# ScalarE copies the first product into the next bank, TensorE adds on top; running sums copied out by ScalarE, accumulators emptied in halves

## The chip, the cores and the metric

The kernel runs on 1 core of one Trainium2 chip. The metric is device time in microseconds (us) of one execution. The engines are TensorE (PE; its weight loads are listed as PEld), VectorE (DVE), ScalarE (ACT), GpSimd (POOL) and SyncE (SP), which issues DMAs. PE writes its products into PSUM, which is used here as eight banks of 128 x 512 fp32: `b0` to `b3` and `o0` to `o3`.

## The reference

Attention with squared ReLU scores over 8 x 3072 tokens, then two mixtures of 8 experts. The change touches only the first mixture, in which every token goes through all experts:

```
x = attn_out.reshape(B * S, D)            # 24576 x 256
logits = x @ w_gate                       # 24576 x 8, then exp and 8 rounds of normalising
for e in range(E):                        # E = 8, F = 1024
    h = np.maximum(x @ w1[e], 0.0)        # 24576 x 1024
    ye = h @ w2[e]                        # 24576 x 256
    out += P[:, e:e + 1] * ye
```

The second mixture routes each token to one expert by an argmax over `x @ emb`; its routing starts while the first mixture still runs.

## The kernel before

All large products are done with fp16 operands split into a high and a low part (three matmuls: high x high, high x low, low x high). The work runs in three stages: attention, the mixture of all experts, the mixture with routing. The middle stage has 768 units. A unit is one expert, two tiles of 512 tokens (1024 tokens) and one quarter of the 1024 hidden features.

**First layer.** `x @ w1` of a unit is a 2 x 2 block product done with seven block products instead of eight (lines 897 to 953). Each block product is three matmuls of 512 columns into one bank. `unit_head` makes four: A11 into `r0`, S1 into `r2`, S2 into `r1`, A22 into `r3`. `unit_tail` makes three more: A12 is added onto `r0`, S4 onto `r2`, S3 onto `r1`. Banks `r0` to `r3` are `b0` to `b3`. ScalarE copies A11 out as `c1` (L920) and S1 as `s5` (L922); VectorE forms the running sums `u2` = S2 + c1 (L926) and `u3` = S2 + S3 + c1 (L946); blocks of the result are `r0`, `c12` = r2 + u2 (L943), and the two halves of `blocks`: r3 + u3 on VectorE (L953) and s5 + u3 on GpSimd (L952). ScalarE applies ReLU and gives the high half in fp16 (L940, L944, L958), VectorE the low half (`low`, L933). A12 and S4 give the part `f0` of the hidden features, `blocks` gives the part `f1`.

**Second layer.** `unit_second(k, q)` multiplies part `q` with `w2`: 24 matmuls of 256 columns into four accumulators `o0` to `o3` (L969), three for each of eight token groups. After the last quarter of the features (`p == 3`) the accumulators are emptied: `evac_begin` has ScalarE read `o0` and `o2` (L1236), `evac_end` has VectorE read `o1` and `o3` (L1252) and GpSimd add what ScalarE copied (L1254).

**Order.** Every engine works through its queue in the order in which the program is written; nothing is rescheduled. The loop over units (L1477 to L1515) is pipelined by one unit: on TensorE stand, in this order, the head of unit k+1 (12 matmuls), the second layer of part `f0` of unit k (24), the tail of unit k+1 (9), the second layer of part `f1` of unit k (24).

**Background.** At four ticks per unit small pieces of other work are put into the queues: normalising of the gates (`sinkhorn`), the routing of finished tiles (`tile_end`), splitting of weights and tiles. One tick stands inside the head, after S1, through the argument `between`. Only this tick may put small products on TensorE, and all of them go to bank `b3`, which `r3` uses too: `pl` (the logits, read by ScalarE at L1123), `pr` (ranks, read by VectorE at L1157 and L1158), `pc` (column sums, read by VectorE at L1035). In L1083 ScalarE squares a finished tile, for which it needs the sum that GpSimd made in L1254.

Of the kernel before, what the change touches and what calls it, by code (L numbers as in the profile page):

```python
# [4 lines left out]
F32 = mybir.dt.float32  # L5
F16 = mybir.dt.float16
I32 = mybir.dt.int32
AF = mybir.ActivationFunctionType
ALU = mybir.AluOpType
AX = mybir.AxisListType  # L10

P = 128
D = 256
E = 8
# [3 lines left out]
TOK = 512  # L18
# [4 lines left out]
SB = 4  # L23
A12, A22, S1, S2, S3, S4, A11 = range(7)
# [62 lines left out]
def program(tc, u, v, z, wg, w1a, w2a, emb, tau, w1b, w2b, out, pool, psum, dram):  # L87
# [575 lines left out]
    with tc.manual_schedule():  # L663
# [167 lines left out]
        def attn_main(i):  # L831
# [24 lines left out]
            if b == B - 1 and qc == QC - 1 and n == 0:  # L856
                load_expert(0)

        moe(tc, dict(locals()))


def moe(tc, st):
# [9 lines left out]
    ones16, ones32, tri16, iota8, half, tokid, itau, emb, out = (  # L872
        g[k] for k in "ones16 ones32 tri16 iota8 half tokid itau emb out".split()
    )
    PE, ACT, DVE, POOL, SP = nc.tensor, nc.scalar, nc.vector, nc.gpsimd, nc.sync
# [3 lines left out]
    terms = []  # L879
    o_ps = {}  # L880
# [3 lines left out]
    def hl_part(i):  # L884

        if not halves:
            t = pool.tile([P, 2, 2, 2 * TOK], F16, name="hl2", tag="z8", bufs=1)
            halves.extend(t[:, j] for j in range(2))
            halves.extend(t.rearrange("p b a q -> p (b a q)").rearrange("p (a q) -> p a q", a=2) for t in hls)
        return halves[i % 4]  # L890

    def product(r, k, blk, part, c, start):
        i, e, p = units[k]
        w = W[i // SB * E + e][0][p // 2]
        x = X[i // 2][part][:, c // 2, c % 2]
        for j, (a, b) in enumerate(((0, 0), (0, 1), (1, 0))):
            PE.matmul(  # L897
                r, lhsT=w[:, p % 2, blk, a, :], rhs=x[:, b, :], start=start and j == 0, stop=j == 2,
                skip_group_check=True,
            )  # L900

    def unit_head(k, between=None):

        i, e, p = units[k]
        sb, t = divmod(i, SB)
        if not terms:
            terms.append(m4([P, 2, TOK], F32, "terms"))
            terms.append(m4([P, 2, TOK], F32, "blocks"))
            terms.append(small("prod5", TOK))
        if i // 2 not in X:  # L910
            bg.finish("x")
        n = sb * E + e
        if t == 0 and p == 1 and n + 1 < NTILE // SB * E:
            load_expert(n + 1)
        if sb + 1 < NTILE // SB and p == 1 and (e, t) in ((4, 0), (7, 2)):
            bg.add("x", load_pair_of_tiles((i + SB) // 2))
        r = live[k] = [bank(j, f"r{j}") for j in range(3)]
        c1, u2, s5 = terms[0][:, 0], terms[0][:, 1], terms[2]
        product(r[0], k, A11, 0, 0, True)
        ACT.activation(out=c1, in_=r[0], func=AF.Copy)  # L920
        product(r[2], k, S1, 1, 0, True)
        ACT.activation(out=s5, in_=r[2], func=AF.Copy)  # L922
        if between:
            between()
        product(r[1], k, S2, 1, 3, True)
        DVE.tensor_tensor(out=u2, in0=r[1], in1=c1, op=ALU.add)  # L926
        r.append(bank(3, "r3"))
        product(r[3], k, A22, 1, 1, True)

    h0, h1 = slice(0, TOK), slice(TOK, 2 * TOK)  # L930

    def low(dst, src, hi, eng=DVE):
        eng.scalar_tensor_tensor(out=dst, in0=src, scalar=0.0, in1=hi, op0=ALU.max, op1=ALU.subtract)  # L933

    def unit_tail(k):

        r = live[k]
        f0, c1, c12 = hl_part(2 * k), terms[0][:, 0], terms[0][:, 1]
        product(r[0], k, A12, 0, 1, False)
        ACT.activation(out=f0[:, 0, h0], in_=r[0], func=AF.Relu)  # L940
        product(r[2], k, S4, 0, 3, False)
        low(f0[:, 1, h0], r[0], f0[:, 0, h0])
        DVE.tensor_tensor(out=c12, in0=r[2], in1=c12, op=ALU.add)  # L943
        ACT.activation(out=f0[:, 0, h1], in_=c12, func=AF.Relu)  # L944
        product(r[1], k, S3, 1, 2, False)
        DVE.tensor_tensor(out=c1, in0=r[1], in1=c1, op=ALU.add)  # L946
        low(f0[:, 1, h1], c12, f0[:, 0, h1])

    def unit_sums(k):
        r = live.pop(k)  # L950
        u3 = terms[0][:, 0]
        POOL.tensor_tensor(out=terms[1][:, 1], in0=terms[2], in1=u3, op=ALU.add)  # L952
        DVE.tensor_tensor(out=terms[1][:, 0], in0=r[3], in1=u3, op=ALU.add)  # L953

    def unit_split(k):
        c2 = terms[1].rearrange("p h q -> p (h q)")
# [1 line left out]
        ACT.activation(out=f1[:, 0], in_=c2, func=AF.Relu)  # L958
        low(f1[:, 1], c2, f1[:, 0])

    def second(hl, f, n, w2t, b0=0):

        for t in range(n // P):
            b = b0 + t // 2
            if f == 0 and t % 2 == 0:
                o_ps[b] = psum.tile([P, 2 * D], F32, name=f"o{b}", tag=f"o{b}", bufs=1)
            o = o_ps[b][:, t % 2 * D:(t % 2 + 1) * D]
            for a, h in ((0, 0), (0, 1), (1, 0)):
                PE.matmul(  # L969
                    o, lhsT=hl[:, a, t * P:(t + 1) * P], rhs=w2t[:, f, h * D:(h + 1) * D],  # L970
                    start=f == 0 and t % 2 == 0 and a + h == 0, stop=f == 7 and a == 1, skip_group_check=True,
                )

    def unit_second(k, q):
        i, e, p = units[k]
        second(hl_part(2 * k + q), 2 * p + q, 2 * TOK, W[i // SB * E + e][1])


    state = {"gates": False}
# [207 lines left out]
    accs = {}  # L1187
# [23 lines left out]
            state["done", i] = True  # L1211
            yield

    parts = []

    def gate(i, e, t):
        return None if i < SB and e < 3 else L[:, 4 * i + t, e:e + 1]

    def target(i, e):

        if e == 0:
            accs[i] = buffer(i)
        elif i < SB and e < 3 and (i, e) not in accs:
            accs[i, e] = buffer(i + SB) if e == 1 else m4([P, 4, D], F32, "y")
        return (accs[i, e] if 0 < e < 3 and i < SB else accs[i]), e == 0 or (i < SB and e < 3)

    def evac_begin(i, e):

        for h in range(2):
            y, new = target(i + h, e)  # L1230
            if not new:
                s = pool.tile([P, TOK], F32, name="r", tag="r", bufs=3).rearrange("p (t d) -> p t d", t=2)
                parts.append((y, s))
            for t in range(2):
                c = gate(i + h, e, t)
                ACT.activation(  # L1236
                    out=y[:, t] if new else s[:, t], in_=o_ps[2 * h][:, t * D:(t + 1) * D], func=AF.Copy,
                    scale=1.0 if c is None else c,
                )

    def evac_end(i, e):
        for h in range(2):
            y, new = target(i + h, e)
            for t in range(2, 4):
                o = o_ps[2 * h + 1][:, (t - 2) * D:(t - 1) * D]
                c = gate(i + h, e, t)
                if c is None:
                    DVE.tensor_copy(out=y[:, t], in_=o)
                elif new:
                    DVE.tensor_scalar(out=y[:, t], in0=o, scalar1=c, scalar2=None, op0=ALU.mult)  # L1250
                else:
                    DVE.scalar_tensor_tensor(out=y[:, t], in0=o, scalar=c, in1=y[:, t], op0=ALU.mult, op1=ALU.add)  # L1252
        for y, s in parts:
            POOL.tensor_tensor(out=y[:, 0:2], in0=y[:, 0:2], in1=s, op=ALU.add)  # L1254
        parts.clear()
        if e == E - 1:
            for h in range(2):
                bg.add("end", tile_end(i + h, accs[i + h]))


    tab = {}
# [74 lines left out]
    def finish_tiles():  # L1336
        bg.finish("end")
# [102 lines left out]
    for k in range(ns):  # L1440
        if k == ns - 120:
            bg.add("prep", embeddings())
        end = (k + 1) % KT == 0
# [33 lines left out]
    for k in range(nu):  # L1477
        i, e, p = units[k]
        if (i, e, p) == (SB, 0, 0):
            g["depth"][0] = 2  # L1480
            bg.lane_rate("w", 6)
            g["plan_weights"](1)
        if i >= NTILE - SB and e == E - 1 and p % 2:
            bg.finish("w")
            if TOK not in tab:
                finish_tiles()
            j = i - (NTILE - SB) + p // 2
            if j < 3:
                load_job_weights(j)
            if i == NTILE - 2 and p == 1:  # L1490
                load_job_rows(0)
        if k + 1 < nu:
            unit_head(k + 1, (lambda: tick_misc(k - 1)) if k else None)
        else:
            for j in range(3, AHEAD_W):
                load_job_weights(j)
            job_first(0)
        unit_split(k)
        unit_second(k, 0)
        tick()  # L1500
        if k + 1 < nu:
            unit_tail(k + 1)
        else:
            job_first(1)
        tick()
        unit_second(k, 1)
        if p == 3:
            evac_begin(i, e)
        if k + 1 < nu:
            unit_sums(k + 1)  # L1510
        else:
            job_first(2)
        if p == 3:
            evac_end(i, e)
        tick()  # L1515


# [39 lines left out]
```

## Time and profile before

| | us |
|---|---|
| median of 3 runs | 10601.97 (10598.34 to 10606.39) |
| profiled execution, its own time | 10603.76 |
| its span, first to last instruction | 10602.0 |
| PE busy | 10453.1 (99%) |
| DVE busy | 6783.1 (64%) |
| ACT busy | 4462.1 (42%) |
| POOL busy | 3512.3 (33%) |
| the 41640 second-layer matmuls, L969 (both mixtures) | 4890.6 busy, 0.9 idle before them |
| the 16128 first-layer matmuls, L897 | 3756.5 busy, 29.1 idle before them |

The granted TensorE clock was 0.996 of full speed over the span. Idle time of an engine is charged to the instruction that comes after it, and to the engine that released that instruction. A busy share of PE says nothing on how fast a matmul runs, so the idle time is what is read here.

### The profile page before, as it was taken

The numbers are of one execution on the slowest core, as the hardware profiler recorded it, in microseconds if no ns is written. First come the engines' busy times: TensorE is split into PE (matmuls) and PEld (weight loads), VectorE is DVE, ScalarE is ACT, GpSimd is POOL, SyncE is SP. The second block draws the span as 40 slices with busy tenths as digits, with TensorE's granted clock in tenths as the row PEclk, the third lists the DMA queues.
The fourth block names the chain that finished last, engine by engine and source line by source line (L and its number), as shares of the span: only waits on it lengthen the run. The fifth ranks groups of instructions, "written<-read, shape, count | busy, mean of one in ns | idle before, by whom it ended". The sixth has DMA issues, their size and how long they took to land. (4 is left out here: it accounts for less than half of the span.)

```text
span 10602.0 us, 193662 instructions
## 1 busy us (share of the span) xinstructions
PE 10453.1 (99%) x78492; PEld 7454.5 (70%) x78492; DVE 6783.1 (64%) x11720; ACT 4462.1 (42%) x8092; POOL 3512.3 (33%) x3094
## 2 busy tenths in 40 slices
PE   8999999999999999999999999999999999999999
PEld 6777777766666666666666666666666666666678
DVE  7676666676667666676766767666666666753333
ACT  5555555334434444443444434344343444433223
POOL 4444445333233333323333323333223332322111
PEclk9999999999999999999999999999999999999999
DMA  8998998311112111111211212112121111115556
GB/s 206 222 224 212 223 222 202 102 38 48 57 52 64 56 58 54 58 58 51 64 56 46 76 42 63 58 49 70 50 53 57 48 47 51 44 62 166 168 186 206
DMA packets 1133187, 1024.67 MB, mean 97 GB/s; under 512 B 853152, under 2 KB 990624, under 8 KB 1102464
## 3 DMA queue, kind: packets, MB, share of 16 engines
q1 hardware_dynamic: 1113520, 960.62, 33.3%
q0 software_dynamic: 18768, 51.67, 1.4%
q8 instruction: 613, 10.04, 0.4%
q14 instruction: 286, 2.34, 0.1%
HBM read 594.27 MB, written 223.93 MB: 77 GB/s over the span
## 5 line engine op out<-in xcount | busy, mean ns | idle before, releaser
L969 PE MATMUL o<-w2t,hl 128*128 128x256 f16 x41640 | 4890.6, 273 | 0.9 <-DVE hl L933 0.6
L969 PEld LDWEIGHTS <-hl 128*128 128x128 f16 x41640 | 4073.8, 98 | 863.1 <-issue 2.1
L897 PE MATMUL r<-xs,w1t 128*128 128x512 f16 x16128 | 3756.5, 379 | 29.1 <-DVE blocks L953 16.9
L952 POOL TENSOR_TENSOR blocks<-prod,terms 128x512 f32<-128x512 f32 x768 | 1336.6, 1740 | 4833.8 <-ACT hl L944 4833.3
L897 PEld LDWEIGHTS <-w1t 128*128 128x128 f16 x16128 | 1567.7, 98 | 1594.1 <-issue 42.6
L933 DVE SCALAR_TENSOR_TENSOR hl<-r,hl 128x512 f16<-128x512 f32 x768 | 531.2, 692 | 1317.7 <-ACT hl L940 1316.6
L940 ACT ACTIVATE hl<-r 128x512 f16<-128x512 f32 x768 | 459.3, 598 | 1997.5 <-PE r L897 1997.3
L933 DVE SCALAR_TENSOR_TENSOR hl<-blocks,hl 128x1024 f16<-128x1024 f32 x768 | 966.6, 1259 | 314.6 <-ACT hl L958 279.5
L920 ACT ACTIVATE terms<-r 128x512 f32<-128x512 f32 x768 | 459.3, 598 | 1342.4 <-PE r L897 819.7
L926 DVE TENSOR_TENSOR terms<-r,terms 128x512 f32<-128x512 f32 x768 | 529.7, 690 | 699.6 <-ACT prod L922 516.5
L944 ACT ACTIVATE hl<-terms 128x512 f16<-128x512 f32 x768 | 485.8, 633 | 1058.9 <-DVE terms L943 1058.9
L958 ACT ACTIVATE hl<-blocks 128x1024 f16<-128x1024 f32 x768 | 809.5, 1054 | 0.0
L776 POOL TENSOR_TENSOR zt<-r 128x512 f32<-128x512 f32 x376 | 427.6, 1138 | 913.8 <-ACT r L771 823.5
L812 PE MATMUL o<-v,hl 128*128 128x256 f16 x6024 | 720.5, 275 | 4.9 <-DVE hl L784 4.9
L1425 DVE SCALAR_TENSOR_TENSOR hl<-h,hl 128x512 f16<-128x512 f32 (+2 forms) x544 | 298.1, 548 | 637.0 <-ACT hl L1424 616.1
L812 PEld LDWEIGHTS <-hl 128*128 128x128 f16 x6024 | 592.4, 99 | 99.8 <-DVE hl L784 5.7
L771 ACT ACTIVATE r<-h 128x512 f32<-128x512 f32 x752 | 439.2, 584 | 504.5 <-PE h L759 498.7
L1419 PE MATMUL h<-xt,w1t 128*128 128x512 f16 (+2 forms) x3264 | 607.7, 322 | 5.3 <-DMA xt<-rows_d 5.3
L784 DVE TENSOR_TENSOR hl<-zt,hl 128x512 f16<-128x512 f32 x502 | 376.7, 759 | 338.9 <-POOL zt L776 192.7
L933 DVE SCALAR_TENSOR_TENSOR hl<-terms,hl 128x512 f16<-128x512 f32 x768 | 532.3, 693 | 77.9
L1424 ACT ACTIVATE hl<-h 128x512 f16<-128x512 f32 (+2 forms) x544 | 263.0, 484 | 695.2 <-PE h L1419 675.4
L946 DVE TENSOR_TENSOR terms<-r,terms 128x512 f32<-128x512 f32 x768 | 523.5, 682 | 0.0
(228 smaller groups left out, 9778.5 us busy)
## 6 DMA issues: line engine op xcount, KB each, us to landing
w1t<-wd SPq DMA_DIRECT2D x192, 896.0 KB
w2t<-wd SPq DMA_DIRECT2D x164, 1024.0 KB
w1t<-wd SPq DMA_DIRECT2D x68, 1024.0 KB
wraw<-in_moe_w SPq DMA_DIRECT2D x112, 512.0 KB
at<-hl SPq DMA_DIRECT2D x216, 256.0 KB
at<-ext SPq DMA_DIRECT2D x104, 256.0 KB
ut<-in_u SPq DMA_DIRECT2D x48, 512.0 KB
xT_d<-xt SPq DMA_DIRECT2D x48, 512.0 KB
```

What stands on the lines that cost most here:

```text
L812: PE.matmul(o, lhsT=tiles[t][a], rhs=vt[:, h * D:(h + 1) * D], start=first and t % 2 == 0 and a + h == 0, stop=last and a == 1, skip_group ...
L897: PE.matmul(r, lhsT=w[:, p % 2, blk, a, :], rhs=x[:, b, :], start=start and j == 0, stop=j == 2, skip_group_check=True,)
L920: ACT.activation(out=c1, in_=r[0], func=AF.Copy)
L926: DVE.tensor_tensor(out=u2, in0=r[1], in1=c1, op=ALU.add)
L933: eng.scalar_tensor_tensor(out=dst, in0=src, scalar=0.0, in1=hi, op0=ALU.max, op1=ALU.subtract)
L940: ACT.activation(out=f0[:, 0, h0], in_=r[0], func=AF.Relu)
L944: ACT.activation(out=f0[:, 0, h1], in_=c12, func=AF.Relu)
L946: DVE.tensor_tensor(out=c1, in0=r[1], in1=c1, op=ALU.add)
L952: POOL.tensor_tensor(out=terms[1][:, 1], in0=terms[2], in1=u3, op=ALU.add)
L958: ACT.activation(out=f1[:, 0], in_=c2, func=AF.Relu)
L969: PE.matmul(o, lhsT=hl[:, a, t * P:(t + 1) * P], rhs=w2t[:, f, h * D:(h + 1) * D], start=f == 0 and t % 2 == 0 and a + h == 0, stop=f == 7 ...
L1419: PE.matmul(h, lhsT=w1t[:, a, c, f * P:(f + 1) * P], rhs=xt[:, 2 * b + c, :], start=i == 0, stop=i == 5)
```

## The change

The sum of A11 and S2 is no longer made by VectorE. ScalarE copies `r0` into the bank `r1` (PSUM to PSUM), and S2 is then added onto it by TensorE, without clearing the bank. What VectorE computed in L926 and L946 is now in the bank, and ScalarE copies it out as `u2` and `u3`. For this S2 moves behind A22 in the head, and S3 moves from the tail to `unit_sums`, which now stands in the middle of the second layer of part `f1`: that is cut into token groups 0 to 3 and 4 to 7. The accumulators are emptied in two halves, `o0`, `o1` after the sums and `o2`, `o3` after the second cut. The work done is otherwise the same.

```diff
 # unit_head
         r = live[k] = [bank(j, f"r{j}") for j in range(3)]
-        c1, u2, s5 = terms[0][:, 0], terms[0][:, 1], terms[2]
+        u2, s5 = terms[0][:, 1], terms[2]
         product(r[0], k, A11, 0, 0, True)
-        ACT.activation(out=c1, in_=r[0], func=AF.Copy)
+        ACT.activation(out=r[1], in_=r[0], func=AF.Copy)
         product(r[2], k, S1, 1, 0, True)
         ACT.activation(out=s5, in_=r[2], func=AF.Copy)
         if between:
             between()
-        product(r[1], k, S2, 1, 3, True)
-        DVE.tensor_tensor(out=u2, in0=r[1], in1=c1, op=ALU.add)
         r.append(bank(3, "r3"))
         product(r[3], k, A22, 1, 1, True)
+        product(r[1], k, S2, 1, 3, False)
+        ACT.activation(out=u2, in_=r[1], func=AF.Copy)
 # unit_tail
...
         ACT.activation(out=f0[:, 0, h1], in_=c12, func=AF.Relu)
-        product(r[1], k, S3, 1, 2, False)
-        DVE.tensor_tensor(out=c1, in0=r[1], in1=c1, op=ALU.add)
         low(f0[:, 1, h1], c12, f0[:, 0, h1])
 # unit_sums
         u3 = terms[0][:, 0]
+        product(r[1], k, S3, 1, 2, False)
+        ACT.activation(out=u3, in_=r[1], func=AF.Copy)
+        DVE.tensor_tensor(out=terms[1][:, 0], in0=r[3], in1=u3, op=ALU.add)
         POOL.tensor_tensor(out=terms[1][:, 1], in0=terms[2], in1=u3, op=ALU.add)
-        DVE.tensor_tensor(out=terms[1][:, 0], in0=r[3], in1=u3, op=ALU.add)
 # second, unit_second
-        for t in range(n // P):
+        for t in range(t0, n // P):
...
-    def unit_second(k, q):
+    def unit_second(k, q, t0=0, n=2 * TOK):
 # evac_begin and evac_end become one function for half h
+    def evac(i, e, h):
+        y, new = target(i + h, e)
...
+        for t in range(2):
+            ACT.activation(
+                out=y[:, t] if new else s[:, t], in_=o_ps[2 * h][:, t * D:(t + 1) * D], func=AF.Copy,
...
+        for t in range(2, 4):
+            o = o_ps[2 * h + 1][:, (t - 2) * D:(t - 1) * D]
...
 # the loop over units
         tick()
-        unit_second(k, 1)
-        if p == 3:
-            evac_begin(i, e)
+        unit_second(k, 1, 0, TOK)
         if k + 1 < nu:
             unit_sums(k + 1)
         else:
             job_first(2)
         if p == 3:
-            evac_end(i, e)
+            evac(i, e, 0)
+        unit_second(k, 1, 4)
+        if p == 3:
+            evac(i, e, 1)
         tick()
```

On TensorE, in a head whose tick holds the logits `pl`, the queue before reads as follows (`r1` takes S2, `r3` takes A22).

```order
L1121 LDWEIGHTS xt_31373
L1121 MATMUL pl_31551<-ew_245,xt_31373 128x8
L897 LDWEIGHTS w1t_30748
L897 MATMUL r1_31541<-xs_28550,w1t_30748 128x512
...
L897 LDWEIGHTS w1t_30748
L897 MATMUL r3_31576<-xs_28550,w1t_30748 128x512
```

And this is the same place in the changed kernel.

```order
L1121 LDWEIGHTS xt_31373
L1121 MATMUL pl_31551<-ew_245,xt_31373 128x8
L897 LDWEIGHTS w1t_30748
L897 MATMUL r3_31572<-xs_28550,w1t_30748 128x512
...
L897 LDWEIGHTS w1t_30748
L897 MATMUL r1_31541<-xs_28550,w1t_30748 128x512
```

The product into `r3`, which shares its bank with `pl`, now stands directly behind `pl`; the three matmuls into `r1` that stood between them come after it.

On ScalarE, around one head in the steady state, the difference is this (L920 copies A11, L922 copies S1, L928 takes `u2`, L951 takes `u3`; L958 is the ReLU of `blocks`).

```order
-L920 ACTIVATE terms_25204<-r0_25388 128x512
+L951 ACTIVATE terms_25204<-r1_25281 128x512
+L920 ACTIVATE r1_25389<-r0_25388 128x512
 L922 ACTIVATE prod5_25206<-r2_25390 128x512
+L928 ACTIVATE terms_25204<-r1_25389 128x512
 L958 ACTIVATE hl1_69<-blocks_25205 128x1024
 L940 ACTIVATE hl2_25253<-r0_25388 128x512
```

L920 now writes a bank, L928 stands ahead of L958, and L951 stands ahead of the next head's L920.

On VectorE, at the end of a unit, the difference is this (L943 makes `c12`, L953 becomes L952 and makes half of `blocks`).

```order
 L943 TENSOR_TENSOR terms_25204<-r2_25282,terms_25204 128x512
-L946 TENSOR_TENSOR terms_25204<-r1_25281,terms_25204 128x512
 L933 SCALAR_TENSOR_TENSOR hl0_68<-terms_25204,hl0_68 128x512
 L552 SCALAR_TENSOR_TENSOR xr_25333<-w_25250,ci_25272,xr_25333 128x2x128 x2
-L953 TENSOR_TENSOR blocks_25205<-r3_25295,terms_25204 128x512
+L952 TENSOR_TENSOR blocks_25205<-r3_25291,terms_25204 128x512
```

L946 is gone, and background work (here L552) still stands ahead of the sum that frees `r3`.

## Rows read from the trace of the kernel before

**Rows 1.** The page, busy time, share of the span and instructions

```profile
PE 10453.1 (99%) x78492; PEld 7454.5 (70%) x78492; DVE 6783.1 (64%) x11720; ACT 4462.1 (42%) x8092; POOL 3512.3 (33%) x3094
```

**Rows 2.** Stretches: start:end, length, busy by engine, clock, DMA share, GB/s

```profile
2050.00:9500.00 7450.00, 7414.55 (x53228) 5120.31 (x53227) 4998.20 (x8183) 3011.06 (x5329) 2384.95 (x1877) 1.00 0.18 54
```

**Rows 3.** Waits, middle stage: who waited for whom, us in total, times, longest

```profile
ACT terms L920 <- DVE blocks L953: 396.0, 180, 3.8
...
ACT junk L1083 <- POOL acc L1254: 19.4, 12, 1.8
...
PE r L897 <- DVE blocks L953: 16.9, 29, 2.0
...
PEld L897 <- DVE base L1158: 15.9, 44, 1.3
...
PE r L897 <- DVE terms L926: 9.6, 1, 9.6
```

**Rows 4.** Timeline of a unit without background: start, length, engine, line

```profile
5013.12 0.63 ACT L944 ACTIVATE hl<-terms 128x512 f16<-128x512 f32 x1 [1.35 <-DVE terms L943]
...
5013.78 0.69 DVE L933 SCALAR_TENSOR_TENSOR hl<-terms,hl 128x512 f16<-128x512 f32 x1
5013.85 1.75 POOL L952 TENSOR_TENSOR blocks<-prod,terms 128x512 f32<-128x512 f32 x1 [5.55 <-ACT hl L944]
5014.39 0.68 DVE L953 TENSOR_TENSOR blocks<-r,terms 128x512 f32<-128x512 f32 x1
...
5014.88 2.75 PE L897 MATMUL r<-xs,w1t 128*128 128x512 f16 x12
5015.78 0.60 ACT L920 ACTIVATE terms<-r 128x512 f32<-128x512 f32 x1 [2.03 <-PE r L897]
...
5016.93 1.05 ACT L958 ACTIVATE hl<-blocks 128x1024 f16<-128x1024 f32 x1
...
5017.47 2.78 PE L969 MATMUL o<-w2t,hl 128*128 128x256 f16 x24
5018.07 1.23 DVE L933 SCALAR_TENSOR_TENSOR hl<-blocks,hl 128x1024 f16<-128x1024 f32 x1 [0.28 <-ACT hl L958]
...
5020.09 2.11 PE L897 MATMUL r<-xs,w1t 128*128 128x512 f16 x9
```

**Rows 5.** Timeline of a head with the logits `pl`

```profile
9182.63 1.46 PE L897 MATMUL r<-xs,w1t 128*128 128x512 f16 x6
9182.98 0.22 ACT L1123 ACTIVATE pgs<-pl 128x64 f32<-128x64 f32 x1
```

**Rows 6.** Line 1123, middle stage: count, ns min/median/max, first and last start

```profile
L1123 ACT ACTIVATE pgs<-pl x44: 219/220/233, 2602.3 to 9183.0; 128x64 f32<-128x64 f32 x44
```

**Rows 7.** Timeline of a head with the ranks `pr`

```profile
9203.16 1.46 PE L897 MATMUL r<-xs,w1t 128*128 128x512 f16 x6
9203.34 0.19 DVE L1157 TENSOR_TENSOR key<-pr,base 128x32 f32<-128x32 f32 x1 [1.56 <-PE pr L1156]
9203.56 0.17 DVE L1158 TENSOR_TENSOR base<-pr,base 128x8 f32<-128x8 f32 x1
```

**Rows 8.** Timeline of a unit in which ScalarE waited at L1083

```profile
3190.41 2.75 PE L897 MATMUL r<-xs,w1t 128*128 128x512 f16 x12
...
3192.82 0.58 ACT L920 ACTIVATE terms<-r 128x512 f32<-128x512 f32 x1
```

**Rows 9.** Timeline of a unit with background ahead of the sum

```profile
3170.38 1.49 DVE L336 SCALAR_TENSOR_TENSOR wout<-wraw,sc,wout 128x256 f16<-128x256 f32 x1
...
3170.87 1.46 PE L897 MATMUL r<-xs,w1t 128*128 128x512 f16 x6
3171.80 0.68 DVE L953 TENSOR_TENSOR blocks<-r,terms 128x512 f32<-128x512 f32 x1
```

**Rows 10.** Line 1134, whole span: count, ns min/median/max

```profile
L1134 DVE TENSOR_TENSOR lg<-lg,xmx x48: 181/1258/1264, 2609.9 to 9813.4; 128x32 f32<-128x32 f32 x48
```

**Rows 11.** Second-layer matmuls, whole span: count, busy, ns, idle before, releasers

```profile
L969 PE MATMUL o<-w2t,hl 128*128 128x256 f16 x41640 | 4890.6, 273 | 0.9 <-DVE hl L933 0.6 <-DVE acc L1252 0.3
```

More of the change, by code (lines that the diff above doesn't have):

```diff
@@ L937, in unit_tail @@
         r = live[k]
-        f0, c1, c12 = hl_part(2 * k), terms[0][:, 0], terms[0][:, 1]
+        f0, c12 = hl_part(2 * k), terms[0][:, 1]
         product(r[0], k, A12, 0, 1, False)
@@ L959, in unit_split, with second @@
         low(f1[:, 1], c2, f1[:, 0])
-    def second(hl, f, n, w2t, b0=0):
-        for t in range(n // P):
+    def second(hl, f, n, w2t, b0=0, t0=0):
+        for t in range(t0, n // P):
             b = b0 + t // 2
@@ L972, in second @@
                 )
-    def unit_second(k, q):
+    def unit_second(k, q, t0=0, n=2 * TOK):
         i, e, p = units[k]
-        second(hl_part(2 * k + q), 2 * p + q, 2 * TOK, W[i // SB * E + e][1])
+        second(hl_part(2 * k + q), 2 * p + q, n, W[i // SB * E + e][1], t0=t0)
     state = {"gates": False}
@@ L1212, in combine_first @@
             yield
-    parts = []
     def gate(i, e, t):
@@ L1225, in target @@
         return (accs[i, e] if 0 < e < 3 and i < SB else accs[i]), e == 0 or (i < SB and e < 3)
[L1227 to L1253, printed above, removed]
+    def evac(i, e, h):
+        y, new = target(i + h, e)
+        if not new:
+            s = pool.tile([P, TOK], F32, name="r", tag="r", bufs=3).rearrange("p (t d) -> p t d", t=2)
+        for t in range(2):
+            c = gate(i + h, e, t)
+            ACT.activation(
+                out=y[:, t] if new else s[:, t], in_=o_ps[2 * h][:, t * D:(t + 1) * D], func=AF.Copy,
+                scale=1.0 if c is None else c,
+            )
+        for t in range(2, 4):
+            o = o_ps[2 * h + 1][:, (t - 2) * D:(t - 1) * D]
+            c = gate(i + h, e, t)
+            if c is None:
+                DVE.tensor_copy(out=y[:, t], in_=o)
+            elif new:
+                DVE.tensor_scalar(out=y[:, t], in0=o, scalar1=c, scalar2=None, op0=ALU.mult)
+            else:
+                DVE.scalar_tensor_tensor(out=y[:, t], in0=o, scalar=c, in1=y[:, t], op0=ALU.mult, op1=ALU.add)
+        if not new:
@@ L1254, in evac_end @@
             POOL.tensor_tensor(out=y[:, 0:2], in0=y[:, 0:2], in1=s, op=ALU.add)
-        parts.clear()
         if e == E - 1:
-            for h in range(2):
-                bg.add("end", tile_end(i + h, accs[i + h]))
+            bg.add("end", tile_end(i + h, accs[i + h]))
     tab = {}
```

## The prediction

> **What bounds the kernel now.** I read the page's busy shares first: PE is busy 99% of the span, no other engine over 64% [rows 1]. As that share can hide slow stretches, I read next the stretch that holds nearly all of the middle stage, 2050 to 9500 us: of its 7450.00 us PE sat idle 7450.00 - 7414.55 = 35.45 us, at full clock [rows 2]. The change keeps all 69 matmuls of a unit (21 into `r`, 48 into `o`), so at best it can take this idle time away; anything it adds ahead of a matmul comes on top. The waits say what the idle time is: A22 waits for the VectorE sum that reads `r3` 29 times, 16.9 us together, and S3 once for 9.6 us [rows 3]. Then I read a unit without background, for how early each input is there.
>
> Write T for the start of a unit's first matmul, 5014.88 in [rows 4]. Twelve first-layer matmuls take 5017.47 - 5014.88 = 2.59 us, 0.216 each; 24 of the second layer 5020.09 - 5017.47 = 2.62 us, 0.109 each [rows 4]. Nine plus twelve plus 48 make a period of 9.77 us without a gap.
>
> **The change part by part.**
>
> *S2 on top of the copy.* S2 is now the fourth product and starts at T + 9 x 0.216 = T + 1.94. The copy L920 starts at T + 0.90 and takes 0.60, so it is done at T + 1.50 [rows 4]. About 0.05 us pass until PE moves on. Margin 0.39 us, cost 0 in a quiet unit. No row has ScalarE writing a bank. Nearest rows: 0.60 to SBUF, and 1.05 for twice the columns (L958) [rows 4]. I take 0.60; at 1.05 S2 would wait 0.90 + 1.05 + 0.05 - 1.94 = 0.06 us in each of 768 units, 46 us. A faster copy gains nothing. The Trainium skill (ScalarE: Activation LUTs, Step-by-step: what each stage is for) holds that ScalarE writes PSUM faster than SBUF; no row here shows it, and by it the copy would cost nothing either.
>
> *S2 no longer stands between the background products and A22.* This is the largest term. `pl`, `pr`, `pc` and `r3` share a bank, so A22 must wait until the background product is read. Today the 0.65 us of S2 cover that. In the head with `pl`, PE goes on with S2 at 9182.63; ScalarE reads `pl` from 9182.98 to 9183.20 [rows 5]. A22 in that place can go at 9183.25: 0.62 us of idle PE. In the head with `pr`, PE goes on at 9203.16 and VectorE has read the ranks at 9203.73, so A22 goes at 9203.78: 0.62 us again [rows 7]. The loads of A22's weights stood waiting for that read 44 times already, hidden behind S2 [rows 3]. `pl` comes 44 times in the stage [rows 6], `pr` 44 times, `pc` 8 times (eight rounds of normalising), which I price alike: 96 x 0.62 = 59.5 us. Behind A22 all of TensorE's queue stands still, so none of it is hidden. It would be nothing only if the readers ran 0.6 us sooner, and they start as soon as their input and the copies ahead of them allow.
>
> *ScalarE's head of line.* S2 now waits for a copy that stands behind background work. At L1083 ScalarE waited for GpSimd 12 times [rows 3]. In one of them L920 ended at 3192.82 + 0.58 = 3193.40, that is T + 2.99 with T = 3190.41 [rows 8]. Before, no matmul needed it so early; now S2 goes at T + 3.04 instead of T + 1.94: 1.10 us, 12 times, 13.2 us.
>
> *The sum that reads `r3`.* A22 needs it at T + 1.30 instead of T + 1.94. In a quiet unit: S3 starts 12 x 0.109 + 0.65 = 1.96 before the next T, its copy L951 0.90 later, from T - 1.06 to T - 0.46; the sum follows at once (a VectorE start came 0.03 after ScalarE's end: 5013.12 + 0.63 to 5013.78) and ends near T + 0.25. Before it ended at 5014.39 + 0.68, T + 0.19 [rows 4]. No cost. With background ahead of it, it is late: in [rows 9] it ended at 3172.48, T + 1.61 with T = 3170.87. Such lateness was met by ScalarE's old wait for L953 180 times [rows 3]. Most of it comes from one thing: L336 took 1.49 us there, and L1134 takes 181 ns at best but 1258 at the median [rows 9, 10], since GpSimd's sum L952 is queued first and these VectorE instructions get on only when it is done. The Trainium skill (Trainium Architecture — The Big Picture, What this means for kernel authors) calls the port that VectorE and GpSimd share an exclusive lock; the 181 against 1258 ns agree. Who comes first decides. Before, GpSimd was queued from T - 1.03 on [rows 4]. Now it must wait for L951, to T - 0.46 plus the 0.10 that it took after L944 (5013.12 + 0.63 to 5013.85), T - 0.36; VectorE's next instruction starts 0.61 after the last `low`, at T - 0.49 [rows 4]. So VectorE should be first by 0.13 us, a single background instruction runs at its own speed, and the sum is in time. Where two such instructions follow each other (L1134 and L1136, in each of the 44 tiles), the second waits for GpSimd's sum, which needs 15.60 - 14.47 = 1.13 us when it is free of the last `low` [rows 4]. From T - 0.30: T + 0.83, then the second 0.2 and the sum 0.68: T + 1.75, and A22 goes 0.5 us late, 44 x 0.5 = 22 us. Bounds: 0 (VectorE keeps the lead for both) and 0.65 each, 29 us.
>
> *What goes.* VectorE loses L926 and L946, ScalarE gains two copies of 0.60. VectorE's 1.37 us per unit are off PE's path. Of the 16.9 + 9.6 us of waits I count 10 as gone: single late sums come in time, but the need is 0.65 earlier, and the 9.6 us stand behind a long stretch of background that the ReLU of `blocks` stands behind as well.
>
> *The ReLU of `blocks` and the cut second layer.* L958 stands behind L928 now. S2 ends its last start at T + 2.59; L928 runs from T + 2.84 to T + 3.44, L958 to T + 4.49, `low` starts 0.09 later and takes 1.23 [rows 4]: T + 5.81. Part `f1` starts at T + 2.59 + 2.62 + 6 x 0.216 = T + 6.51 instead of T + 7.16. The margin falls from 2.7 us (today `low` ends at 5018.07 + 1.23, T + 4.42) to 0.7 us. Cost 0; if a GpSimd instruction holds `low` back for its 1.13 us, 0.4 us in that unit. Emptying the accumulators in halves gains nothing: PE waited 0.3 us for them in the whole run [rows 11]. Both cuts of the second layer add no matmul.
>
> *Sum.* 59.5 + 13.2 + 22 - 10 = 84.7 us on the profiled execution's 10603.76 us (span 10602.0, the rest lies around it): 10688. That execution lies 1.8 us above the median of the runs, so 10687 is forecast, 0.8% slower. A difference of over 0.2% (21 us) can be told from none.
>
> **The rivals.**
>
> *A. GpSimd still comes first (0.18).* The lead of 0.13 us is small and rests on sums of three latencies. Then the sum ends at T + 1.61 as in [rows 9] in the 180 units, and A22 goes at T + 1.66 instead of T + 1.30: 180 x 0.36 = 65 us, beside the 44 double ones. 10687 + 65 = 10752. For it: it came first in every such unit before. Against it: it now starts from the same copy as VectorE's sum.
>
> *B. The copy between banks is slow (0.05).* At the upper bound of 1.05 us: 10687 + 46 = 10733.
>
> *C. Costs as above, but most waits go (0.12).* The double instructions cost nothing, L1083 clears earlier, and 26.5 us of waits go, with up to the 15.9 us of waiting loads [rows 3]: 59.5 - 42.4 = 17 us, 10619. No change that can be measured.
>
> *D. Faster (0.05).* VectorE's lighter queue takes away all 35.45 us of idle PE [rows 2], and nothing comes in their place: 10602 - 35 = 10567. It decides by one point: A22 must find its bank read when it arrives, 0.62 us sooner than `pl` and `pr` were read in [rows 5, 7]. For it: VectorE's queue is 1.37 us shorter. Against it: `pl` is read by ScalarE, and the rank reader already waited for PE [rows 7].
>
> **How the numbers follow.** The forecast has 0.60 (its own range 10645 to 10720, from the bounds 0 and 29 of the doubles and 0 to 26.5 us of waits that go), A 0.18, B 0.05, C 0.12, D 0.05. For 8 in 10 the range goes over A to 10785, with both A and part of B, and down into C, to 10615; D and the rest of C lie outside. Faster by over 0.2%: D, 0.05. Within: C, 0.12. Slower: 0.83.
>
> **What would show it.** PE waiting for L1123 and for L1158 before A22, some 44 times each and about 0.6 us each, is the main term; without them the forecast is wrong. PE waiting for L920 about 12 times by 1.1 us. PE waiting for the sum L952 some 44 times (forecast) or near 200 times (A). L1134's median near 0.2 us says that VectorE came first, near 1.2 us that GpSimd did. L920's mean tells B. PE should wait for the `low` of `blocks` almost never.

## The result, and the profile after

The changed kernel took 10722.5 us (median of 4 runs, 10719.85 to 10730.48) against 10604.2 us before (4 runs): a ratio of 1.0114, 95% interval 1.0096 to 1.0131. The profiled execution has a span of 10719.9 us against 10602.0. Forecast was 10687 us, range 10615 to 10785.

The page's busy line and the stretch that answers to [rows 2] (length, then busy us by engine) show where the time lies:

```profile
PE 10479.1 (98%) x78492; PEld 7461.9 (70%) x78492; DVE 5685.3 (53%) x10184; ACT 5346.1 (50%) x9628; POOL 3138.1 (29%) x3094
```

```profile
2050.00:9600.00 7550.00, 7431.63 (x53193) 5125.59 (x53192) 3920.51 (x6672) 3876.77 (x6831) 2021.52 (x1878) 1.00 0.17 53
```

VectorE's busy time fell by 1098 us (1536 instructions fewer), ScalarE's rose by 884 (1536 more), and GpSimd's fell by 374 with as many instructions as before: its sum of `blocks` took 1.75 us in the unit of [rows 4] and takes 1.27 in the unit below. The time went up all the same: PE's idle time in the stretch rose from 35.45 us to 118.37. What PE waited for there, by line (us in total, times, longest), answers to [rows 3]:

```profile
PE r L897 <- DVE blocks L952: 46.9, 66, 1.9
PE r L897 <- DVE base L1158: 22.9, 44, 1.5
PE r L897 <- ACT pgs L1123: 21.0, 44, 0.5
PE r L897 <- ACT r L920: 12.7, 12, 1.3
PE o L969 <- DVE hl L933: 8.3, 3, 6.4
PE pr L1151 <- DVE blocks L952: 3.6, 3, 2.5
PE o L969 <- ACT hl L958: 3.5, 2, 2.9
PE r L897 <- DVE cs L1035: 2.0, 8, 0.3
```

Idle time counts less than the delay, since the row of a first-layer matmul is 0.379 us long and the next starts after 0.216, so that two rows overlap by 0.16 us. So I also took the delay from the starts of the matmuls: the time from the start before to a product's first start, less the usual step of the one before (0.216 or 0.109 us in the layers, 0.015 in the small products), kept where it is over 0.03 us. Over the stage, from the first unit's start to the last's, it comes to this:

| | before | after |
|---|---|---|
| stage, first unit to last | 7583.9 | 7695.0 |
| period of a unit, median | 9.773 | 9.773 |
| A22 behind `pl` / `pr` / `pc` | 0 | 27.7 / 29.6 / 4.0 |
| A22 behind a first-layer product: the sum that reads `r3` is late | 26.8 | 62.9 in 92 heads |
| S2 (before: behind `pc`; after: behind the copy L920) | 0.8 | 18.7 in 32 heads |
| S3 | 9.7 | 0.1 |
| second layer | 5.1 | 15.8 |
| small products that wait for the sum that reads `r3` | 11.0 | 4.5 |

The stage is 111.1 us longer of 117.9 in the span, and the rows of the table rise by 110 together. The rest lies outside the stage: it starts 1.8 us later, and from the start of its last unit to the end it takes 5.1 us more.

A unit without background, at offsets like those of [rows 4], with T = 5043.98 (start, length, engine, line):

```profile
5042.22 0.63 ACT L944 ACTIVATE hl<-terms 128x512 f16<-128x512 f32 x1 [1.36 <-DVE terms L943]
...
5042.87 0.60 ACT L951 ACTIVATE terms<-r 128x512 f32<-128x512 f32 x1
5042.88 0.69 DVE L933 SCALAR_TENSOR_TENSOR hl<-terms,hl 128x512 f16<-128x512 f32 x1 [0.70 <-ACT hl L944]
5043.50 0.69 DVE L952 TENSOR_TENSOR blocks<-r,terms 128x512 f32<-128x512 f32 x1
5043.54 1.27 POOL L953 TENSOR_TENSOR blocks<-prod,terms 128x512 f32<-128x512 f32 x1 [8.50 <-ACT terms L951]
5043.98 2.75 PE L897 MATMUL r<-xs,w1t 128*128 128x512 f16 x12
5044.89 0.58 ACT L920 ACTIVATE r<-r 128x512 f32<-128x512 f32 x1 [1.42 <-PE r L897]
...
5047.26 1.05 ACT L958 ACTIVATE hl<-blocks 128x1024 f16<-128x1024 f32 x1
5048.41 1.23 DVE L933 SCALAR_TENSOR_TENSOR hl<-blocks,hl 128x1024 f16<-128x1024 f32 x1 [4.22 <-ACT hl L958]
...
5050.48 1.47 PE L969 MATMUL o<-w2t,hl 128*128 128x256 f16 x12
```

The copy is done at T + 1.49 (forecast T + 1.50), u3 is copied from T - 1.11 (forecast T - 1.06), the sum L952 ends at T + 0.21 (T + 0.25), `low` of `blocks` at T + 5.66 (T + 5.81), ahead of part `f1` at T + 6.50. Nothing waits here, as forecast. VectorE's queue goes on at 5043.50, GpSimd's sum starts at 5043.54. Which of the two comes first is decided by as little as that, and in this unit, without background, it costs nothing either way.

The head with `pl`, which answers to [rows 5]. Before, S2 went on 1.70 us after the head's first matmul and `pl` was read from 2.05 us after it: [rows 5] have 9182.63 and 9182.98, and the head began with this row.

```profile
9180.93 1.46 PE L897 MATMUL r<-xs,w1t 128*128 128x512 f16 x6
```

A22, which now stands in that place, would have started at 9290.41 + 1.70 and starts at 9292.73, 0.62 us late:

```profile
9290.41 1.46 PE L897 MATMUL r<-xs,w1t 128*128 128x512 f16 x6
...
9292.46 0.22 ACT L1123 ACTIVATE pgs<-pl 128x64 f32<-128x64 f32 x1
9292.73 1.46 PE L897 MATMUL r<-xs,w1t 128*128 128x512 f16 x6 [0.48 <-ACT pgs L1123]
```

The unit that answers to [rows 8]: ScalarE waits for GpSimd at L1083, the copy follows, and S2 goes at T + 3.14 instead of T + 1.94 (T = 3212.33):

```profile
3212.33 2.10 PE L897 MATMUL r<-xs,w1t 128*128 128x512 f16 x9
...
3214.43 0.42 ACT L1083 ACTIVATE junk<-acc 128x256 f32<-128x256 f32 x1 [1.15 <-POOL acc L1246]
...
3214.85 0.58 ACT L920 ACTIVATE r<-r 128x512 f32<-128x512 f32 x1
...
3215.47 0.81 PE L897 MATMUL r<-xs,w1t 128*128 128x512 f16 x3 [1.04 <-ACT r L920]
```

And the unit with two background instructions ahead of the sum:

```profile
5275.21 0.18 DVE L1134 TENSOR_TENSOR lg<-lg,xmx 128x32 f32<-128x32 f32 x1
5275.26 1.26 POOL L953 TENSOR_TENSOR blocks<-prod,terms 128x512 f32<-128x512 f32 x1 [9.25 <-ACT terms L951]
5275.31 1.27 DVE L1136 SCALAR_TENSOR_TENSOR key<-key,iota 128x32 f32<-128x32 f32 x1
...
5275.70 2.99 PE L897 MATMUL r<-xs,w1t 128*128 128x512 f16 x12
5276.50 0.68 DVE L952 TENSOR_TENSOR blocks<-r,terms 128x512 f32<-128x512 f32 x1
```

L1134 runs at its own 0.18 us, GpSimd starts, and L1136 is on its engine until GpSimd is done. The twelve matmuls take 2.99 us instead of 2.75: A22 waited 0.24 us inside them.

This is the order in 33 of the 44 tiles. In the other 11 GpSimd is first, by 0.07 to 0.08 us, and L1134 is held as it was before the change:

```profile
3262.75 0.63 ACT L944 ACTIVATE hl<-terms 128x512 f16<-128x512 f32 x1 [1.74 <-DVE terms L943]
3263.29 0.58 ACT L951 ACTIVATE terms<-r 128x512 f32<-128x512 f32 x1
3263.41 0.69 DVE L933 SCALAR_TENSOR_TENSOR hl<-terms,hl 128x512 f16<-128x512 f32 x1 [0.69 <-ACT hl L944]
3263.94 1.28 POOL L953 TENSOR_TENSOR blocks<-prod,terms 128x512 f32<-128x512 f32 x1 [1.67 <-ACT terms L951]
3264.02 1.26 DVE L1134 TENSOR_TENSOR lg<-lg,xmx 128x32 f32<-128x32 f32 x1
```

In all 11 the copy L951 follows L944 at once and starts 0.54 us after it, in the other 33 it starts 0.65 us after it; `low` starts 0.66 us after L944 in all 44. So GpSimd, which needs the copy, is ahead of VectorE, which goes on after `low`. Over all kinds of background the sum L952 is late in 78 heads in which VectorE was first (47.9 us) and in 14 in which GpSimd was (15.0 us).

### The profile page after: what moved, and what is told of

It reads as the page before. It is cut to its first block, busy times and chain, and to the rows that moved or that the text cites. A ratio compares the mean times of both kernels' runs of the same rounds, so it can differ in the third digit from the quotient of the medians.

```text
span 10719.9 us, 192891 instructions
## 1 busy us (share of the span) xinstructions
PE 10479.1 (98%) x78492; PEld 7461.9 (70%) x78492; DVE 5685.3 (53%) x10184; ACT 5346.1 (50%) x9628; POOL 3138.1 (29%) x3094
## 5 line engine op out<-in xcount | busy, mean ns | idle before, releaser
L969 PE MATMUL o<-w2t,hl 128*128 128x256 f16 x41640 | 5014.8, 273 | 11.8 <-DVE hl L933 8.3
L897 PE MATMUL r<-xs,w1t 128*128 128x512 f16 x16128 | 3894.6, 379 | 109.1 <-DVE blocks L952 46.9
L953 POOL TENSOR_TENSOR blocks<-prod,terms 128x512 f32<-128x512 f32 x768 | 989.5, 1288 | 5347.2 <-ACT terms L951 5211.3
L944 ACT ACTIVATE hl<-terms 128x512 f16<-128x512 f32 x768 | 483.4, 629 | 1066.6 <-DVE terms L943 1066.6
L920 ACT ACTIVATE r<-r 128x512 f32<-128x512 f32 x768 | 448.2, 584 | 726.8 <-PE r L897 726.5
L958 ACT ACTIVATE hl<-blocks 128x1024 f16<-128x1024 f32 x768 | 804.9, 1048 | 0.0
L928 ACT ACTIVATE terms<-r 128x512 f32<-128x512 f32 x768 | 458.6, 597 | 564.5 <-PE r L897 563.7
L1409 PE MATMUL h<-xt,w1t 128*128 128x512 f16 (+2 forms) x3264 | 607.7, 322 | 10.4 <-DMA xt<-rows_d 10.3
L952 DVE TENSOR_TENSOR blocks<-r,terms 128x512 f32<-128x512 f32 x768 | 526.8, 686 | 1.2 <-ACT terms L951 1.2
```

What stands on the lines that cost most here:

```text
L897: PE.matmul(r, lhsT=w[:, p % 2, blk, a, :], rhs=x[:, b, :], start=start and j == 0, stop=j == 2, skip_group_check=True,)
L920: ACT.activation(out=r[1], in_=r[0], func=AF.Copy)
L928: ACT.activation(out=u2, in_=r[1], func=AF.Copy)
L969: PE.matmul(o, lhsT=hl[:, a, t * P:(t + 1) * P], rhs=w2t[:, f, h * D:(h + 1) * D], start=f == 0 and t % 2 == 0 and a + h == 0, stop=f == 7 ...
L1409: PE.matmul(h, lhsT=w1t[:, a, c, f * P:(f + 1) * P], rhs=xt[:, 2 * b + c, :], start=i == 0, stop=i == 5)
```

## The experiments

Ratios are against the kernel before on the same chip; the chips of the experiments took 10609.6 to 10631.1 us for it. Stage means first unit's start to last unit's start, from each run's profile.

**The tick ahead of S1.** In `unit_head`:

```diff
         ACT.activation(out=r[1], in_=r[0], func=AF.Copy)
+        if between:
+            between()
         product(r[2], k, S1, 1, 0, True)
         ACT.activation(out=s5, in_=r[2], func=AF.Copy)
-        if between:
-            between()
```

> The changed kernel (10722.5 us) with the head's background tick moved ahead of S1, so that S1 stands between the products pl, pr, pc and A22. Theory 1 (A22 waits for the readers of the shared bank because nothing covers them): the three waits of A22, 27.7 us behind pl, 29.6 us behind pr and 4.0 us behind pc, fall to under 6 us together, the wait for the sum L952 stays near 63 us, the time is about 10667 us. Theory 2 (the readers are late by what their engines have queued, the place of the products hardly matters): A22's waits stay above 45 us and the time within 15 us of 10722.

Ratio 1.0067 (1.0050 to 1.0084), stage 7644.8 us, 50 us shorter than the change. PE's waits, by line:

```profile
PE r L897 <- DVE blocks L952: 45.7, 66, 1.9
PE r L897 <- ACT r L920: 12.7, 12, 1.3
PE o L969 <- DVE hl L933: 7.7, 3, 5.8
PE pr L1151 <- DVE blocks L952: 5.5, 3, 3.1
PE r L897 <- DVE base L1158: 4.7, 10, 0.8
```

The wait for L1123 is gone, that for L1158 is down from 44 times to 10, and the wait for the sum stays at 66. By the starts of the matmuls, A22's delay in heads with one of the three products fell from 61.3 us to 8.2, of which 8.0 stand in 20 heads whose ranks are read later still. That is not the under 6 us expected, but it is theory 1: 0.65 us of matmuls between a small product and A22 cover most of its readers.

**The sums ahead of the tick.** In the loop over units:

```diff
-        tick()
         unit_second(k, 1, 0, TOK)
         if k + 1 < nu:
             unit_sums(k + 1)
         else:
             job_first(2)
+        tick()
```

> The changed kernel with the tick that stood ahead of the cut second layer moved behind the sums, so that VectorE makes the sum that reads r3 ahead of the background. Theory 1 (A22 waits in 90 heads because two or more background instructions stand ahead of the sum): PE's wait for L952 falls from 62.9 us to under 5 us, the waits for L1123 and L1158 stay near 57 us, the time is about 10660 us. Theory 2 (the copy L951 is what makes the sum late): the wait for L952 stays and the time is within 15 us of 10722.

Ratio 1.0067 (1.0050 to 1.0084), stage 7640.3 us, 55 us shorter. A22's delay behind first-layer products fell from 62.9 to 3.1 us; `pl` cost what it did, `pr` 32.3 us instead of 29.6. Theory 1 holds. Not foreseen: L920 was waited for 37 times instead of 12 (S2's delay 25.5 us, up from 18.7), as ScalarE's share of that tick now stands closer ahead of the copy.

**Both moves.**

> Both moves, the tick behind A11 and the sums ahead of the other tick. If the two costs are separate they add: about 10722.5 - 55 - 62 = 10605 us, the same as before the change, with the wait for L920 (18.7 us in 32 heads) left over. If one hides in the other, the time is above 10630 us.

Ratio 1.0026 (1.0015 to 1.0036), stage 7599.8 us: 95 us of the 105 that the two gave singly (50 + 55), and of the 117 expected. They nearly add. What is left is mostly the copy (S2's delay 29.7 us) and A22 (20.1 us: 13.7 in 22 heads in which the ranks' reader is late, by nearly 1 us in 12 of them, and 6.4 behind the sum).

**Only the halves.** In the kernel before, `second` cut in two and `evac` in two, with S3 and the sums as they were:

```diff
-        unit_second(k, 1)
-        if p == 3:
-            evac_begin(i, e)
+        unit_second(k, 1, 0, TOK)
         if k + 1 < nu:
             unit_sums(k + 1)
         else:
             job_first(2)
         if p == 3:
-            evac_end(i, e)
+            evac(i, e, 0)
+        unit_second(k, 1, 4)
+        if p == 3:
+            evac(i, e, 1)
```

> The kernel before with only the cut second layer and the accumulators emptied in halves, sums and products in their old places. Theory 1 (this part neither costs nor gains, PE hardly waited for accumulators): 10604 us, within 10 us, PE's waits as before. Rival (the cut costs TensorE a pause at each of the 1536 new borders between kinds of matmuls, or the later emptying makes the next unit wait): 10630 us or more.

Ratio 1.000 (0.9991 to 1.0010), stage 7582.4 us. This part of the change neither costs nor gains.

**Before, with A22 ahead of S2.**

```diff
-        product(r[1], k, S2, 1, 3, True)
-        DVE.tensor_tensor(out=u2, in0=r[1], in1=c1, op=ALU.add)
         r.append(bank(3, "r3"))
         product(r[3], k, A22, 1, 1, True)
+        product(r[1], k, S2, 1, 3, True)
+        DVE.tensor_tensor(out=u2, in0=r[1], in1=c1, op=ALU.add)
```

> The kernel before with one edit: A22 ahead of S2; VectorE still makes u2 and u3. The stage from the first unit to the last lasted 7583.9 us before and 7695.0 us with the whole change. Theory A (order of A22 alone brings the bank waits, about 61 us; and with u3 made by VectorE, GpSimd is queued first and every background instruction is held, so single ones make the sum late too): A22 waits for L953 in more than 200 heads, about 110 us; the stage is about 7733 us, the time 149 us above before. Theory B (VectorE would run single background instructions in time here too, only pairs are late, as in the changed kernel): waits in about 90 heads, 63 us, stage about 7681 us, 97 us above before.

Ratio 1.0142 (1.0125 to 1.0159), stage 7733.8 us: theory A, to 1 us. A22's delay is 63.4 us behind the three small products and 111.8 us behind the sum, in 250 heads. So the order of A22 alone costs more than the whole change. With u3 made by VectorE, GpSimd's sum is queued first and holds even single background instructions. The same instruction, L1166, which stands alone ahead of the sum in most of its units, in this run (first) and with the whole change (second); count, then ns min/median/max:

```profile
L1166 DVE SCALAR_TENSOR_TENSOR row<-xab,gt x44: 1227/1232/1243, 2672.1 to 9386.6; 128x4 f32<-128x4 f32 x44
```

```profile
L1166 DVE SCALAR_TENSOR_TENSOR row<-xab,gt x44: 157/160/163, 2647.2 to 9321.4; 128x4 f32<-128x4 f32 x44
```

**The change, with S2 ahead of A22.**

```diff
+        product(r[1], k, S2, 1, 3, False)
+        ACT.activation(out=u2, in_=r[1], func=AF.Copy)
         r.append(bank(3, "r3"))
         product(r[3], k, A22, 1, 1, True)
-        product(r[1], k, S2, 1, 3, False)
-        ACT.activation(out=u2, in_=r[1], func=AF.Copy)
```

> The changed kernel with S2 ahead of A22 again (S2 still added onto ScalarE's copy). Theory (S2 at T + 1.30 needs a copy that is done at T + 1.48 and seen 0.03 us later): S2 waits about 0.21 us in every unit, 161 us; A22's waits for the shared bank fall from 61 to under 6 us and those for L952 from 63 to about 15 us; the stage is about 7755 us against 7695. Rival (the copy's result is seen late enough only in units with background): under 60 us of waits for L920, stage below 7660 us.

Ratio 1.0172 (1.0155 to 1.0189), stage 7759.4 us. The median period of a unit is 10.014 us, 0.241 longer: the twelve matmuls of a head now take 3.00 us. The theory holds; the stage came out as expected because two misses cancel. S2's delay is 203 us in 670 heads, not 161, and A22's is 4.4 us in all, not some 20. The heads with small products between S1 and S2 do not wait for the copy.

```profile
5048.09 3.00 PE L897 MATMUL r<-xs,w1t 128*128 128x512 f16 x12
5050.93 2.78 PE L969 MATMUL o<-w2t,hl 128*128 128x256 f16 x24
```

So A22 was not put first for nothing: S2 on top of a copy needs A22 as cover, and the background products need S2. One product cannot cover both; in the head there is S1 besides, which the first experiment uses.

**Both moves, and the last tick behind the copy.** The tick at the end of the loop goes into the next head's `between`:

```diff
-            unit_head(k + 1, (lambda: tick_misc(k - 1)) if k else None)
+            unit_head(k + 1, (lambda: (tick(), tick_misc(k - 1))) if k else None)
         else:
+            tick()
...
             evac(i, e, 1)
-        tick()
```

> Both moves of ticks as in the run with both, and the last tick of a unit moved into the next head behind L920, so that no background stands ahead of the copy that S2 needs. Theory (the waits for L920 come from background ahead of it on ScalarE): they fall from 22 us to under 2 us, the stage from 7600 to about 7575 us, the time is then within 10 us of before. Rival (what is moved is waited for elsewhere, at L922 or at the ReLU of blocks): the stage stays above 7590 us.

Ratio 0.9994 (0.9985 to 1.0004), stage 7569.2 us. S2's delay fell to 0.6 us. With the three moves the changed kernel is where the kernel before was. That it takes three moves to get there is the price of the change: A22 is still 18.4 us late in this run, and the kernel before gains from one such move too (last experiment: stage 7554.1 us, 15 us shorter than this one).

**The second sum on VectorE.**

```diff
-        POOL.tensor_tensor(out=terms[1][:, 1], in0=terms[2], in1=u3, op=ALU.add)
+        DVE.tensor_tensor(out=terms[1][:, 1], in0=terms[2], in1=u3, op=ALU.add)
```

> The changed kernel with the sum of s5 and u3 (L953) made by VectorE behind L952 instead of by GpSimd, so that GpSimd holds nothing at the end of a unit. Theory 1 (the second of two background instructions is late because it waits for GpSimd's sum): L1136 falls from 1267 to near 180 ns, the wait of PE for L952 from 63 us to under 20 us, the stage from 7695 to about 7650 us, although VectorE has 0.7 us more work per unit. Theory 2 (it is simply too much VectorE work ahead of the sum): the wait stays above 50 us or grows, stage 7690 us or more.

Ratio 1.0067 (1.0050 to 1.0084), stage 7650.7 us. L1136 at its own pace, and PE waits for the sum 10 times, for 10.3 us:

```profile
L1136 DVE SCALAR_TENSOR_TENSOR key<-key,iota x44: 183/185/189, 2648.1 to 9280.5; 128x32 f32<-128x32 f32 x44
```

Theory 1 holds: more VectorE work, less delay. One delay grew: A22's behind `pr` went from 29.6 to 38.1 us.

**Before, with the sums ahead of the tick.** The same move in the kernel before:

```diff
-        tick()
         unit_second(k, 1)
         if p == 3:
             evac_begin(i, e)
         if k + 1 < nu:
             unit_sums(k + 1)
         else:
             job_first(2)
+        tick()
         if p == 3:
             evac_end(i, e)
```

> The kernel before with one edit: the tick ahead of the second layer of part f1 moved behind the sums L952 and L953. Theory (the wait of A22 for the sum is the background ahead of it on VectorE, with the change or without it): A22's 26.8 us of waits before the change and the 5.7 us of the ranks' products for L953 fall to under 6 us, S3's single wait of 9.7 us stays, the stage falls from 7583.9 to about 7557 us and the time by about 0.25%, below both kernels. Rival (the background moved behind the sums is then late for what needs it, or the copies that wait behind it hold S2 or the ReLU of blocks): the stage stays above 7575 us and the time within 0.1%.

Ratio 0.9974 (0.9965 to 0.9983), 10580.3 us against 10609.6 on its chip, stage 7554.1 us. A22's delay fell from 26.8 to 5.5 us, S3's stayed at 9.9. This one beats both kernels. PE's longest waits that are left:

```profile
PE r L897 <- DVE terms L926: 9.6, 1, 9.6
PE r L897 <- DVE base L1158: 3.3, 2, 2.7
```

## Why the prediction came out as it did

The direction, the place and most sizes were right; the sum fell short by 33 us, 85 us for 118.

- *S2 no longer covers the readers of the shared bank*: 59.5 us forecast, 61.3 measured: 0.63 us each behind `pl`, 0.67 behind `pr`, 0.50 behind `pc`, where 0.62 was worked out for all. The experiment with the tick ahead of S1 takes 53 us of it away.
- *The copy between banks*: 0 forecast in a quiet unit, 0 measured. Rival B is out: L920 takes 0.58 us in the unit shown, not longer than to SBUF.
- *ScalarE's head of line*: 13.2 us forecast for the 12 units of L1083, 14.5 measured (12 times 1.2). Missed: 20 more heads of 0.2 us, 4.2 us, in which copies for the accumulators stand ahead of L920 together with a background copy (L1096, 10 heads), with L1083 (9) or with L951 (1).
- *The sum that reads `r3`*: this is the term that was mis-sized. Its mechanism is shown: none of the 223 heads with a single background instruction ahead of the sum was late (9 were before), L1134's median fell from 1258 to 186 ns, and the second of two waited for GpSimd (L1136: 1267 ns), which the run without GpSimd's sum takes away.

```profile
L1134 DVE TENSOR_TENSOR lg<-lg,xmx x44: 182/186/1262, 2626.2 to 9300.7; 128x32 f32<-128x32 f32 x44
L1136 DVE SCALAR_TENSOR_TENSOR key<-key,iota x44: 178/1267/1286, 2627.4 to 9300.8; 128x32 f32<-128x32 f32 x44
```

  The 44 heads with L1134 and L1136 cost 23.4 us, forecast 22, but that they agree is luck. In 26 of them the case is the one that was priced, and A22 is 0.24 us late, not 0.5: 6.2 us. In 7 a third instruction (L262 or L336) stands there too, 5.3 us. In the other 11 GpSimd was first, 11.9 us: rival A was right there, and wrong for the 180 units that it was priced for. (The 0.5 was also added up wrong: 0.83 + 0.2 + 0.68 is 1.71, not 1.75.) And these 44 are not the only ones. In 48 more heads two or more other instructions stand there: L1109 with L1110 and L649 in 11 heads (9.8 us), the three of the normalising in 7 (9.1 us), most of the others a weight split L336 behind another instruction. They cost 39.5 us, and I counted none of them. Two instructions do not always make the sum late: of 141 heads that have two or more, 92 were. Nor did the waits of before shrink beside the new ones: the forecast had them 10 us smaller, together a net of 12 us; it was 36.1 (26.8 to 62.9).
- *The wait of S3*: the prediction left the 9.6 us in place, and the time did stay, in another place: S3 waits no more, and the second layer's delay rose by 10.7 us. Of this 9.6 us lie within 15 us of where S3 waited (at 2242 us of the span), where part `f1` waits for the ReLU L958 (3.0) and for its `low` (6.6) behind the same stretch of background.
- *The halves*: 0 forecast, 0 measured alone.
- *Rival D* needed the readers to come 0.6 us sooner. They started when they did before: L1123 at T + 2.05 in both profiles. *Rival C* needed the waits of before to go; they grew.

The remaining 6.8 us outside the stage were not looked into.

## What to carry to other kernels

Where one engine is busy without a gap, read what each of its instructions covers: moving one product by one place here uncovered the readers of three small products and a sum that was often late, and the wait is what the product used to hide. A lighter VectorE gained nothing here; the order of the queues ahead of what the busy engine needs did, and moving the needed sum ahead of background work paid with the change and without it. When counting the places where a queue holds two background instructions ahead of a needed one, count all kinds, not the pair that the profile happens to show.

## What the runs showed of the hardware

- ScalarE's copy from bank to bank took 0.58 us, the same form to SBUF 0.60 (L920, after and before, in the two units without background). The Trainium skill (ScalarE: Activation LUTs, Step-by-step: what each stage is for) says that ScalarE writes PSUM faster; the trace agrees, by 0.016 us, where ScalarE had been idle before the copy (medians 582 ns of 570 copies and 598 ns of 747). Where the copy followed another instruction at once there was no gain: 582 ns into the bank, 579 ns to SBUF (197 and 20 copies). Adding a product onto it cost TensorE nothing: 0.216 us a matmul as before.
- A VectorE instruction of 4 columns (L1166) took 160 ns where it started 0.05 to 0.06 us ahead of GpSimd's sum (all 44 times after the change) and 1232 ns where GpSimd's sum was first (the run with A22 ahead of S2). L1134 after the change took about 185 ns in the 33 units where it started 0.05 to 0.07 us ahead, and over 1250 ns in the 11 where it started 0.07 to 0.08 us behind.
- Between the end of a copy on ScalarE and the matmul that needs it lay 0.05 us (L920 and S2 in the 12 heads of L1083).
